# Block 0 of a windowed attention with a gated FFN: scores and PV by 64-key tiles in eight steps

## The chip, the cores and the metric

The kernel runs on one core of a Trainium2 chip. A core has five engines with queues of their own, which meet only through semaphores: TensorE (PE, with its weight loads PEld), VectorE (DVE), ScalarE (ACT), GpSimd (POOL) and SyncE (SP), which here only issues DMAs. TensorE reads SBUF and writes PSUM (eight banks of 128 x 512 float32). The metric is the device time of one execution in microseconds (us), as a median over runs. The trace is one execution taken by the hardware profiler. A line such as L656 is a line of the kernel as it was before the change.

## The reference

The input `x` has 2048 rows of 448 in bfloat16. It is normalized once, and two branches read the result: attention with 16 heads of 28, in which a query sees itself and the 255 keys before it, and a gated FFN of width 1792. Both are added to `x`.

```python
xn = _layernorm(x)
q, k, v = split(xn @ wqkv)                      # 16 heads of 28
scores = einsum("bhqd,bhkd->bhqk", q, k) * 28 ** -0.5
mask = (q_idx - k_idx >= 0) & (q_idx - k_idx < 256)
o = softmax(where(mask, scores, -1e9)) @ v
return x + o.reshape(B, S, D) @ wo + (gelu(xn @ w_gate) * (xn @ w_up)) @ w_down
```

## The kernel before

The rows are worked in four blocks of 512 queries (`qb` 0 to 3). Every queue runs in the order in which the program issues instructions; the order is written out by hand, and nothing is reordered. In each block there are two stages.

*Attention* (`attention`, L617). The heads are worked in four groups `g` of four. A list of steps (`steps_of`, L559) tells which key tiles are scored together. One step scores up to 512 columns for four heads (L684, TensorE, tile `sc`, four PSUM banks of which there is one set), takes the exp of all of it in one ScalarE instruction (L688, tile `p_sb`, five buffers in a ring), and zeroes what lies outside the window. Scores are kept with keys on partitions and queries on columns; the softmax has no maximum, and its denominator comes from a column of ones in `v_sb`. `pv(g)` (L648) multiplies the finished `p_sb` of a group by `v_sb` into PSUM (tile `ov`), and brings it to SBUF as `oc`. `sums` (L625) transposes `oc` on VectorE and takes reciprocals, `inverse` (L633) spreads them, and `scale_o` (L622) multiplies on GpSimd into `oN`.

Blocks 1 to 3 score tiles of 64 keys in two halves of the partitions, in ten steps. Their masks are products with stored 0/1 tiles on VectorE (`apply_masks`, L597, at the start of the step after), and their PV has a bank for each half of the keys: ScalarE copies one to `oc` and VectorE adds the other (`add_halves`, L639). The add of the last group is put off to `flush` (L644).

Block 0 has its own steps: nine, of tiles of 128 keys. Their masks are `affine_select` on GpSimd right after the exp (`masked`, L606), their PV has one bank, copied by VectorE (L666).

Between the steps TensorE is fed other work, from a list `plan` with one entry for each step (L842 for block 0). `(u, 7)` means seven pieces of the generator `u`; a string names one of the functions above. In block 0, `u` is first the projections of groups 1 to 3 (`gen_qk`), then the up projection of five of the seven pairs of FFN columns, in the order p = 1, 2, 3, 0, 4 (`gen_up`, L495: seven pieces a pair; after the seventh, two casts from the tile `ue` to `hT`, both on VectorE, or, for a `p` in `shared`, one on each of VectorE and ScalarE). `w` is the values and projections of block 1 (`gen_pairs`): pairs v0, v2, k0, k1, k2, of seven pieces each. `stat` and `rstd` are the row statistics, `fill_pads` small GpSimd copies into the padding columns of weights. In steps 1 to 3, `ahead`, `ahead2` and `ahead3` normalize rows for the next block on VectorE (L170) and issue DMAs.

PSUM has four spare banks, b0 to b3, in a first-in-first-out list (`take`, `give`, L203): each pair of projections or of FFN columns takes two. A tile on a bank waits until the readers of the tile before it are done.

*FFN* (`gated`, L509). For each `p` a gate projection of 14 matmuls (`gate`, tile `gt`, two sets of two banks, the same PSUM as `sc`), its gelu on ScalarE (L528), and the product with the up projection on VectorE: for `p` in `early` with the stored `hT` (L533), otherwise with PSUM (L536). In block 0 the pairs 0 to 4 are early, so that five gates come one after the other. `gate(0)` also calls `last_v`, which is `rest` (L713): the masks still open, `pv(2)` and `pv(3)`. After each pair, `hook` (L879) issues what belongs to other stages: after pair 0 `sums` of what is open, after pair 1 `inverse`, after pair 4 of block 0 three DMAs of `oN` on the ScalarE queue (`o_collect`, L347, L884). Then ScalarE loads the tables of exp (L899), and the next block's scores take the PSUM of the gates.

Of the kernel before, what the change touches and what calls it, by code (L numbers as in the profile page):

```python
# [27 lines left out]
def kernel(  # L28
# [462 lines left out]
    def both(hT, p):  # L491

        return hT[:, :, :].rearrange("q (h k) n -> q h k n", h=2)[:, :, p, :]
# [15 lines left out]
    def gated(qb, early, last_v, flush, hook):  # L509

        hT = hTs[qb]
        us, ges = {}, {}

        def up(p):
            if p in early:
                return
            us[p] = [take("u") for _ in range(2)]
            for c in range(7):
                chunk(us[p], wu, p, qb, c)

        def gate(p):
            gt = phase[0].pool.tile([P, 2, QB], f32, name="gt", tag="s")
            for c in range(7):
                chunk([gt[:, i, :] for i in range(2)], wg, p, qb, c)
            if not p:
                last_v()
            ges[p] = work.tile([P, 4, QB], bf16, name="p_sb", bufs=5)[:, 0:2, :]
            nc.scalar.activation(out=ges[p][:, :, :], in_=gt[:, :, :], func=ACT.Gelu_apprx_tanh)  # L528

        def end(p):  # L530
            ge = ges.pop(p)
            if p in early:
                nc.vector.tensor_tensor(out=both(hT, p), in0=ge[:, :, :], in1=both(hT, p), op=ALU.mult)  # L533
# [24 lines left out]

    def steps_of(qb):  # L559

        k = 4 * qb
        if not qb:
            def four(g):
                return [(g, None, 3, 384, 128, 0), (g, None, 0, 0, 384, 128)], 512, [(None, (0,), 2 * P, True), (None, (384,), P, False)]

            for g in (0, 2):  # L570
                yield four(g)
                if not g:
                    yield [(0, None, 1, 128, 384, 0), (0, None, 2, 256, 128, 384)], 512, [(None, (0, 384), P, True), (None, (256,), P, False)]
                    yield [(0, None, 2, 384, 128, 0), (1, None, 0, 0, 384, 128)], 512, [(None, (128,), P, True), (None, (384,), P, False)]
                    yield [(1, None, 3, 384, 128, 0), (1, None, 1, 128, 384, 128)], 512, [(None, (0,), 2 * P, True), (None, (384,), P, False)]
                    yield [(1, None, 2, 256, 256, 0), (2, None, 2, 256, 256, 256)], 512, [(None, (0, 256), P, True)]
                else:
                    yield [(2, None, 1, 128, 384, 0), (3, None, 3, 384, 128, 384)], 512, [(None, (0, 384), P, True), (None, (256,), P, False)]
                    yield [(3, None, 0, 0, 384, 0), (3, None, 2, 384, 128, 384)], 512, [(None, (0,), P, True), (None, (256,), P, False)]
                    yield [(3, None, 1, 128, 384, 0), (3, None, 2, 256, 128, 384)], 512, [(None, (0, 384), P, True), (None, (256,), P, False)]  # L580
            return

        def first(g):
            return ([(g, 0, k, 0, 320, 0), (g, 1, k, 64, 320, 0), (g, 0, k - 1, 0, 192, 320), (g, 1, k + 2, 320, 192, 320)], 512, 0)

        def second(g):
            return ([(g, 0, k + 1, 128, 320, 0), (g, 1, k + 1, 192, 320, 0), (g, 0, k + 3, 384, 128, 320), (g, 1, k + 3, 448, 64, 320),
                     (g, 1, k - 2, 0, 128, 384), (g, 0, k - 2, 0, 64, 448)], 512, 1)

        for g in (0, 2):  # L590
            yield first(g)
            yield second(g)
            yield [(g + i, h, k + 2 - 3 * h, 256 - 256 * h, 256, 256 * i) for i in range(2) for h in range(2)], 512, 2
            yield first(g + 1)
            yield second(g + 1)

    def apply_masks(p_sb, i):  # L597

        cols = [c for c, *_ in EDGES[i]]
        for js in ((0,), (1, 2), (3,)):  # L600
            w = 64 * len(js)
            reg = p_sb[:, :, cols[js[0]]:cols[js[0]] + w]
            m = masks[:, i, js[0]:js[-1] + 1, :].rearrange("p a b -> p (a b)").unsqueeze(1).to_broadcast([P, 4, w])
            nc.vector.tensor_tensor(out=reg, in0=reg, in1=m, op=ALU.mult)  # L604

    def masked(p_sb, half, cols, w, diag):  # L606
        r = slice(0, P) if half is None else slice(64 * half, 64 * half + 64)
        for c in cols:
            reg = p_sb[r, :, c:c + w]
            mid = [[0, 4]]  # L610
            if w > P:
                reg = reg.rearrange("p h (b q) -> p h b q", q=P)
                mid.append([0, w // P])
            nc.gpsimd.affine_select(out=reg, in_=reg, pattern=mid + [[1 if diag else -1, min(w, P)]], compare_op=ALU.is_ge, fill=0.0,  # L614
                                    base=0 if diag else -1, channel_multiplier=-1 if diag else 1)

    def attention(qb, plan):  # L617
        oN = blk.tile([P, 4, QB], bf16, name="oN")
# [19 lines left out]

        def add_halves(oc, ov):  # L639
            nc.scalar.copy(out=oc[:, :], in_=ov[0][:, :])  # L640
            nc.vector.tensor_tensor(out=oc[:, :], in0=oc[:, :], in1=ov[1][:, :], op=ALU.add)  # L641
            give(*ov)

        def flush():  # L644
# [2 lines left out]

        def pv(g):  # L648

            ov = [take("ov") for _ in range(2 if qb else 1)]  # L650
            todo = parts.pop(g)
            for n, (half, kt, q0, nq, col, p_sb) in enumerate(todo):
                k0 = 64 * half if half else 0
                r = slice(k0, k0 + (P if half is None else 64))
                for j in range(4):
                    nc.tensor.matmul(ov[half or 0][32 * j:32 * j + 32, q0:q0 + nq], lhsT=v_sb[r, kt, 4 * g + j, :],  # L656
                                     rhs=p_sb[r, j, col:col + nq], start=n == (half or 0), stop=n + len(ov) >= len(todo),
                                     tile_position=(k0, 32 * j), skip_group_check=True)
            oc = work.tile([P, QB], f32, name="oc", tag="wb" if g % 2 else "wa", bufs=1)
            if qb:  # L660
                if g > 2:
                    behind.append((oc, ov))
                else:
# [8 lines left out]
        for i, (scores, ncol, edges) in enumerate(steps):  # L672
# [5 lines left out]
            ss = phase[0].pool.tile([P, 4, QB], f32, name="sc", tag="s")  # L678
            p_sb = work.tile([P, 4, QB], bf16, name="p_sb", bufs=5)
            for g, half, kt, q0, nq, col in scores:  # L680
                k0, nk = (64 * half, 64) if half is not None else (0, P)
                for j in range(4):
                    r = slice(32 * j, 32 * j + Dh)
                    nc.tensor.matmul(ss[k0:k0 + nk, j, col:col + nq], lhsT=kT[r, g, kt * P + k0:kt * P + k0 + nk],  # L684
                                     rhs=qT[r, g, ring(qb).start + q0:ring(qb).start + q0 + nq], start=True, stop=True,
                                     tile_position=(32 * j, k0), skip_group_check=True)
                parts.setdefault(g, []).append((half, kt, q0, nq, col, p_sb))
            nc.scalar.activation(out=p_sb[:, :, 0:ncol], in_=ss[:, :, 0:ncol], func=ACT.Exp, scale=SCALE)  # L688
# [143 lines left out]
    for qb in range(NB):  # L832
# [4 lines left out]
        if qb == 0:  # L837
            new_hT(0)
            early = (0, 1, 2, 3, 4)
            u = chain(gen_qk((1, 2, 3), {1: (3, pvs[3]), 2: (2, pvs[2])}), gen_up(0, (1, 2, 3, 0, 4), (3, 4)))  # L840
            w = gen_pairs(1, (("v", 0), ("v", 2), ("k", 0), ("k", 1), ("k", 2)))
            plan = [[(u, 2), ahead, (u, 1)], [lambda: v_dense(2, pvs[2]), (u, 2), ahead2, (u, 1)],  # L842
                    [lambda: spare.append(spare.pop(1)), (u, 2), ahead3, (u, 4)], [lambda: stat(8), (u, 11)],
                    [lambda: stat(9), (u, 7), lambda: stat(10), (u, 7), lambda: fill_pads(True)], ["sums", (u, 7)],
                    ["inverse", "scale", (w, 11)], [(w, 10)],
                    [lambda: stat(11), (w, 7), lambda: rstd(8, 4), "sums", "inverse", (w, 7)]]
        else:
            d = gen_down(qb - 1)
            if qb < 3:
# [209 lines left out]
```

## Time and profile before

| what | us |
|---|---|
| time, median of 3 runs (212.6 to 213.0) | 212.84 |
| the profiled execution's own time | 212.69 |
| its span, first to last instruction | 210.8 |
| PE busy | 205.1 (97%) |
| DVE busy | 157.8 (75%) |
| ACT busy | 132.0 (63%) |
| POOL busy | 48.4 (23%) |
| the 39 exps (L688), 1878 ns each | 73.2 |
| the 21 selects of block 0 (L614) | 14.2 |

The granted TensorE clock is 1.000 of full speed throughout. Block 0's first scores start at 11.2 us, its last at 33.6; block 1's first start at 51.9.

How to read the rows: in the timeline a row is the start, the length, the engine, the line, the operation, output and input with shapes, and how many instructions were merged. In brackets is the idle time of that engine before it, and what ended it by the profile; where the engine named was done long before, it was something else. "ACTq" and "SPq" are the queues that issue DMAs. Rows of the chain of waits are the start, the length, and what held the end of the kernel in that time. A row of a table of stretches gives the stretch, its length, then for PE, PEld, DVE, ACT and POOL the busy time and the instructions, then the clock, the DMA share and GB/s. Matmuls are pipelined, and two or four of them run in different rows of the array at once, so busy times of one matmul overlap with those of the next.

### The profile page before, as it was taken

The page shows a single profiled execution, that of the slowest core. Times are in us where ns is not written, and L with a number is a line of the kernel's source. Part 1 is how long each engine was busy: PE and PEld are TensorE (multiplying, and loading weights), DVE is VectorE, ACT ScalarE, POOL GpSimd, SP SyncE. Part 2 cuts the span into 40 slices and gives each one's busy share as a digit, 9 for nine tenths or more (in the row PEclk, how much of TensorE's full clock was granted, in tenths as well). Part 3 has the DMA queues.
Part 4 walks back from the last instruction along what each step waited for, and adds up shares of the span by engine and source line. Part 5 has one row for each costly group of instructions (what it writes and reads, how often), then busy time and mean ns, then how long its engine had stood idle before and what let it go on. Part 6 is the DMA issues. An engine that isn't in the chain of part 4 may idle for free.

```text
span 210.8 us, 6335 instructions
## 1 busy us (share of the span) xinstructions
PE 205.1 (97%) x2678; PEld 96.5 (46%) x2682; DVE 157.8 (75%) x356; ACT 132.0 (63%) x124; POOL 48.4 (23%) x83
## 2 busy tenths in 40 slices
PE   7899999999999999999999999999999999999994
PEld 2333444444444445444445444544444454544562
DVE  6899998999788985696438897395385699659722
ACT  4699588566777977413778788523587787757000
POOL 5388658451000220040000112013000022005100
PEclk9999999999999999999999999999999999999999
DMA  6999989959411001003421000100100010100011
GB/s 176 275 223 230 107 215 220 218 175 234 110 48 48 22 5 39 7 3 71 75 75 47 25 0 27 23 0 15 32 3 0 5 47 0 48 3 0 22 59 41
DMA packets 24889, 15.67 MB, mean 74 GB/s; under 512 B 9208, under 2 KB 24728, under 8 KB 24856
## 3 DMA queue, kind: packets, MB, share of 16 engines
q1 hardware_dynamic: 23814, 14.87, 31.7%
q8 instruction: 22, 0.36, 0.7%
q10 hardware_dynamic: 1042, 0.34, 0.6%
q14 instruction: 11, 0.09, 0.1%
HBM read 9.26 MB, written 2.41 MB: 55 GB/s over the span
## 4 chain that ended last, share of the span: by engine, by line
PE 94%; DVE 2%; ACT 1%; DMA 1%; issue 1%; DVEq 0%; ACTq 0%
PE po L394 24%; PE gt L488 20%; PE u L488 12%; PE ue L488 8%; PE sc L684 7%; PE pq L333 7%; PE ov L656 5%; PE pv L319 4%; PE pq L190 2%; PE pl L394 2%; DVE st L155 1%; PE po L403 1%; DMA x_sb<-in_A_x_dram 1%; PE pv L190 1%; ACT p_sb L688 1%; PE s L190 1%
## 5 line engine op out<-in xcount | busy, mean ns | idle before, releaser
L688 ACT ACTIVATE p_sb<-sc 128x2048 bf16<-128x2048 f32 x39 | 73.2, 1878 | 20.0 <-PE sc L684 14.0
L528 ACT ACTIVATE p_sb<-gt 128x1024 bf16<-128x1024 f32 x28 | 28.7, 1025 | 33.6 <-PE gt L488 30.7
L623 POOL TENSOR_TENSOR oN<-oc,l 128x512 bf16<-128x512 f32 x16 | 21.9, 1374 | 117.9 <-DVE l L636 117.9
L488 PE MATMUL gt<-xnT,wg 64*128 64x512 bf16 x224 | 45.6, 376 | 0.0
L394 PE MATMUL po<-wd,hT 128*128 128x448 bf16 x210 | 43.3, 353 | 0.0
L488 PE MATMUL gt<-xsw,wg 64*128 64x512 bf16 x168 | 40.7, 376 | 0.0
L536 DVE TENSOR_TENSOR hT<-p_sb,u 128x512 bf16<-128x512 bf16 x34 | 21.9, 677 | 15.9 <-PE u L488 15.7
L604 DVE TENSOR_TENSOR p_sb<-p_sb,masks 128x256 bf16<-128x256 bf16 (+1 forms) x90 | 27.9, 365 | 7.5 <-ACT p_sb L688 7.5
L394 PEld LDWEIGHTS <-hT 128*128 128x128 bf16 x238 | 21.8, 98 | 19.5 <-issue 2.4
L488 PEld LDWEIGHTS <-wg 64*128 64x128 bf16 x392 | 19.0, 94 | 22.5 <-issue 0.2
L488 PEld LDWEIGHTS <-wu 64*128 64x128 bf16 x392 | 18.7, 94 | 22.5 <-issue 0.8
L488 PE MATMUL u<-xnT,wu 64*128 64x512 bf16 x136 | 28.1, 376 | 0.0
L488 PE MATMUL u<-xsw,wu 64*128 64x512 bf16 x102 | 24.7, 376 | 0.0
L488 PE MATMUL ue<-xnT,wu 64*128 64x512 bf16 x88 | 18.0, 377 | 0.0
L684 PE MATMUL sc<-qT,kT 28*64 28x320 bf16 (+7 forms) x648 | 16.4, 261 | 0.1
L488 PE MATMUL ue<-xsw,wu 64*128 64x512 bf16 x66 | 16.4, 377 | 0.0
L614 POOL TENSOR_SCALAR_AFFINE_SELECT p_sb<-p_sb 128x512 bf16<-128x512 bf16 (+1 forms) x21 | 14.2, 703 | 6.0 <-ACT p_sb L688 5.9
L641 DVE TENSOR_TENSOR oc<-oc,ov 128x512 f32<-128x512 f32 x12 | 8.2, 681 | 9.1 <-ACT oc L640 9.0
L684 PEld LDWEIGHTS <-kT 28*64 28x64 bf16 (+1 forms) x648 | 7.5, 102 | 13.3 <-issue 12.0
L382 DVE TENSOR_TENSOR res<-po,x_sb 128x448 bf16<-128x448 f32 x13 | 7.7, 621 | 7.7 <-PE po L403 4.4
L505 DVE CAST hT<-ue 128x512 bf16<-128x512 f32 x17 | 11.0, 678 | 1.3 <-PE ue L488 1.2
L170 DVE TENSOR_SCALAR xn<-x_sb,mv_all,rstd_all 128x448 bf16<-128x448 bf16 (+1 forms) x28 | 11.0, 434 | 0.3 <-ACT rstd_all L161 0.3
(111 smaller groups left out, 281.2 us busy)
## 6 DMA issues: line engine op xcount, KB each, us to landing
out_dram<-res SPq DMA_DIRECT2D x15, 112.0 KB
wd<-in_B_w_down_dram SPq DMA_DIRECT2D x2, 784.0 KB
x_sb<-in_A_x_dram SPq DMA_DIRECT2D x3, 448.0 KB
xsw<-xnT SPq DMA_DIRECT2D x6, 192.0 KB
wu<-in_B_w_up_dram SPq DMA_DIRECT2D x4, 224.0 KB
wg<-in_B_w_gate_dram SPq DMA_DIRECT2D x2, 448.0 KB
wu<-in_B_w_up_dram SPq DMA_DIRECT2D x2, 336.0 KB
wg<-in_B_w_gate_dram SPq DMA_DIRECT2D x2, 336.0 KB
```

The lines of the kernel that those rows point to most:

```text
L170: nc.vector.tensor_scalar(out=xf[:, lo:lo + n], in0=x_sb[:, t, src:src + n], scalar1=mv_all[:, t, 0:1], scalar2=rstd_all[:, t:t + 1], op0= ...
L333: nc.tensor.matmul(ps, lhsT=w.rearrange("p h d -> p (h d)"), rhs=xchunk(qb, hi, c, qb * QB, QB), start=c == 0, stop=c == 6, tile_position= ...
L394: nc.tensor.matmul(po[:, 0:w], lhsT=x[:, k, tt * P:(tt + 1) * P], rhs=wt[:, k, lo:up], start=start and n == 0, stop=stop and n == len(term ...
L488: nc.tensor.matmul(ps, lhsT=w[64 * hi:64 * hi + 64, c, p * P:(p + 1) * P], rhs=xchunk(qb, hi, c, qb * QB, QB), start=c == 0, stop=c == 6, ...
L505: copy(out=hTs[qb][:, p + 7 * i, :], in_=us[i])
L528: nc.scalar.activation(out=ges[p][:, :, :], in_=gt[:, :, :], func=ACT.Gelu_apprx_tanh)
L536: nc.vector.tensor_tensor(out=hT[:, p + 7 * i, :], in0=ge[:, i, :], in1=u, op=ALU.mult)
L604: nc.vector.tensor_tensor(out=reg, in0=reg, in1=m, op=ALU.mult)
L614: nc.gpsimd.affine_select(out=reg, in_=reg, pattern=mid + [[1 if diag else -1, min(w, P)]], compare_op=ALU.is_ge, fill=0.0, base=0 if diag ...
L623: nc.gpsimd.tensor_tensor(out=oN[:, g, :], in0=oc[:, :], in1=inv, op=ALU.mult)
L684: nc.tensor.matmul(ss[k0:k0 + nk, j, col:col + nq], lhsT=kT[r, g, kt * P + k0:kt * P + k0 + nk], rhs=qT[r, g, ring(qb).start + q0:ring(qb) ...
L688: nc.scalar.activation(out=p_sb[:, :, 0:ncol], in_=ss[:, :, 0:ncol], func=ACT.Exp, scale=SCALE)
```

## The change

Block 0 gets tiles of 64 keys, as the later blocks have them, in two steps for each group, eight in all. In the second step of a group, one more matmul by four heads fills the columns 384 to 512 of the lower half, which hold no score; it is not used in PV.

The masks of steps 1 to 4 stay on GpSimd: now six selects a step, each of 64 partitions by four heads by 64 columns. Those of steps 5 to 8 go to VectorE, with two of the three products that a step of the later blocks has; as there, they are issued at the start of the following step, and those of step 8 in `rest`.

PV of every group has two banks, with a copy on ScalarE and an add on VectorE (448 of the 512 columns, since the upper half of the keys adds nothing to the first 64 queries). The one of group 3 is put off to `flush`, which is now also called after the product of an early pair.

The fills of TensorE are laid out anew over eight steps, with the same pieces in the same order, and of the pair p = 2, which comes second, one cast goes to ScalarE.

```diff
@@ gated / end(p)
             if p in early:
                 nc.vector.tensor_tensor(out=both(hT, p), in0=ge[:, :, :], in1=both(hT, p), op=ALU.mult)
+                flush()
@@ steps_of(0)
-            def four(g):
-                return [(g, None, 3, 384, 128, 0), (g, None, 0, 0, 384, 128)], 512, [(None, (0,), 2 * P, True), (None, (384,), P, False)]
...
-                    yield [(3, None, 1, 128, 384, 0), (3, None, 2, 256, 128, 384)], 512, [(None, (0, 384), P, True), (None, (256,), P, False)]
+            for g in range(4):
+                yield [(g, 0, 0, 0, 320, 0), (g, 1, 0, 64, 320, 0), (g, 0, 2, 256, 192, 320), (g, 1, 2, 320, 192, 320)], 512, 1
+                yield [(g, 0, 1, 128, 320, 0), (g, 1, 1, 192, 320, 0), (g, 0, 3, 384, 128, 320), (g, 1, 3, 448, 64, 320),
+                       (g, 0, 2, 448, 64, 448), (g, None, 3, 384, 128, 384)], 512, 1
@@ apply_masks, masked
-    def apply_masks(p_sb, i):
+    def apply_masks(p_sb, i, n):
-        for js in ((0,), (1, 2), (3,)):
+        for js in ((0,), (1, 2), (3,))[0:n]:
...
+    def masked(p_sb):
+        for hi in range(2):
+            reg = p_sb[64 * hi:64 * hi + 64].rearrange("p h (b q) -> p h b q", q=64)
+            for part, kind in ((reg[:, :, 0], 1), (reg[:, :, 5], 1), (reg[:, :, 4], -1)):
+                nc.gpsimd.affine_select(out=part, in_=part, pattern=[[0, 4], [kind, 64]], compare_op=ALU.is_ge, fill=0.0, base=min(kind, 0),
+                                        channel_multiplier=-kind)
@@ add_halves
-            nc.vector.tensor_tensor(out=oc[:, :], in0=oc[:, :], in1=ov[1][:, :], op=ALU.add)
+            q0 = 0 if qb else 64
+            nc.vector.tensor_tensor(out=oc[:, q0:], in0=oc[:, q0:], in1=ov[1][:, q0:], op=ALU.add)
@@ pv
-            ov = [take("ov") for _ in range(2 if qb else 1)]
+            ov = [take("ov") for _ in range(2)]
...
-            if qb:
-                if g > 2:
-                    behind.append((oc, ov))
-                else:
-                    add_halves(oc, ov)
+            if g > 2:
+                behind.append((oc, ov))
             else:
-                nc.vector.tensor_copy(out=oc[:, :], in_=ov[0][:, :])
-                give(*ov)
+                add_halves(oc, ov)
@@ attention, each step
-            if qb:
-                fresh.append((p_sb, edges))
+            if qb or i > 3:
+                fresh.append((p_sb, edges, 3 if qb else 2))
             else:
-                for m in edges:
-                    masked(p_sb, *m)
+                masked(p_sb)
@@ plan of block 0
-            u = chain(gen_qk((1, 2, 3), {1: (3, pvs[3]), 2: (2, pvs[2])}), gen_up(0, (1, 2, 3, 0, 4), (3, 4)))
+            u = chain(gen_qk((1, 2, 3), {1: (3, pvs[3]), 2: (2, pvs[2])}), gen_up(0, (1, 2, 3, 0, 4), (2, 3, 4)))
...
-                    [lambda: stat(9), (u, 7), lambda: stat(10), (u, 7), lambda: fill_pads(True)], ["sums", (u, 7)],
-                    ["inverse", "scale", (w, 11)], [(w, 10)],
-                    [lambda: stat(11), (w, 7), lambda: rstd(8, 4), "sums", "inverse", (w, 7)]]
+                    [lambda: stat(9), (u, 7), lambda: stat(10), (u, 5), lambda: fill_pads(True)], ["sums", (u, 9)],
+                    ["inverse", "scale", (w, 17)],
+                    [lambda: stat(11), (w, 4), lambda: rstd(8, 4), "sums", "inverse", (w, 14)]]
```

More of the change, by code (lines that the diff above doesn't have):

```diff
@@ L604, in apply_masks @@
             nc.vector.tensor_tensor(out=reg, in0=reg, in1=m, op=ALU.mult)
[L606 to L615, printed above, removed]
+    def masked(p_sb):
[4 more added lines that the diff above has]
+                                        channel_multiplier=-kind)
     def attention(qb, plan):
@@ L648, in pv @@
         def pv(g):
[L650 removed]
+            ov = [take("ov") for _ in range(2)]
             todo = parts.pop(g)
             for n, (half, kt, q0, nq, col, p_sb) in enumerate(todo):
[L653 to L654 removed]
+                k0 = 64 * half
+                r = slice(k0, k0 + 64)
                 for j in range(4):
[L656 to L657 removed]
+                    nc.tensor.matmul(ov[half][32 * j:32 * j + 32, q0:q0 + nq], lhsT=v_sb[r, kt, 4 * g + j, :],
+                                     rhs=p_sb[r, j, col:col + nq], start=n == half, stop=n + 2 >= len(todo),
                                      tile_position=(k0, 32 * j), skip_group_check=True)
             oc = work.tile([P, QB], f32, name="oc", tag="wb" if g % 2 else "wa", bufs=1)
[L660 to L667 removed]
+            if g > 2:
+                behind.append((oc, ov))
+            else:
+                add_halves(oc, ov)
             copied.append((g, oc))
@@ L680, in attention @@
             for g, half, kt, q0, nq, col in scores:
-                k0, nk = (64 * half, 64) if half is not None else (0, P)
+                fills = half is None
+                half = 1 if fills else half
+                k0, nk = 64 * half, 64
                 for j in range(4):
@@ L686, in attention @@
                                      tile_position=(32 * j, k0), skip_group_check=True)
-                parts.setdefault(g, []).append((half, kt, q0, nq, col, p_sb))
+                if not fills:
+                    parts.setdefault(g, []).append((half, kt, q0, nq, col, p_sb))
             nc.scalar.activation(out=p_sb[:, :, 0:ncol], in_=ss[:, :, 0:ncol], func=ACT.Exp, scale=SCALE)
             flush()
-            if qb:
-                fresh.append((p_sb, edges))
-            else:
-                for m in edges:
-                    masked(p_sb, *m)
+            if qb or i > 3:
+                fresh.append((p_sb, edges, 3 if qb else 2))
+            else:
+                masked(p_sb)
             while later:
```

9 lines of the change are left out of this document (removed).

## The prediction

> **What bounds the kernel now.** I read the page first, then the busy time of each engine in stretches of block 0, then the chain that ended last, then each engine's timeline from 9 to 56 us.
>
> ```profile
> PE 205.1 (97%) x2678; PEld 96.5 (46%) x2682; DVE 157.8 (75%) x356; ACT 132.0 (63%) x124; POOL 48.4 (23%) x83
> 26.00:35.00 9.00, 9.00 (x116) 3.75 (x116) 7.58 (x15) 6.95 (x5) 6.52 (x13) 1.00 0.95 214
> 41.00:50.00 9.00, 9.00 (x86) 4.20 (x84) 8.93 (x17) 4.86 (x5) 3.50 (x3) 1.00 0.75 225
> ```
>
> The first row is the page's, the others are stretches (us, then PE, PEld, DVE, ACT, POOL busy). PE is busy 97% of the span and all the time in block 0, so time goes down only with PE's own work, and goes up with any wait put on PE. The second engine to look at is DVE: it has 1.42 us free between 26 and 35, and 0.07 us between 41 and 50. The change adds DVE work in the first of these and a wait in the second, so its place is what matters.
>
> **PE's own work.** From the chain that ended last (start, us, what):
>
> ```profile
> 22.05 0.61 PE ov L656 x20
> 22.65 0.33 PE sc L684 x8
> 22.98 3.13 PE ue L488 x28
> 28.06 0.60 PE ov L656 x16
> 37.15 1.51 PE gt L488 x14
> 38.66 1.10 PE ov L656 x36
> 61.28 1.32 PE pv L319 x14
> 81.60 1.26 PE ov L656 x81
> 155.57 0.34 PE sc L684 x16
> 168.70 0.66 PE ov L656 x40
> 169.36 0.36 PE sc L684 x16
> ```
>
> A step's scores take 0.33 now. The later blocks already use 64-key tiles: 0.34 and 0.36, I take 0.35. Seven pairs take 1.51 (gt), so fourteen take 3.02; the ue stretch has 3.13, so each change over costs 0.11. One step less saves 0.33+0.11 = 0.44, and eight steps at 0.02 more cost 0.16: -0.28 us. PV of a group in block 3 streams 1280 columns in each half in 0.66. The new one streams 1024 and 896 in its halves; 512 columns take 1.51/7 = 0.216, so 256 fewer are 0.11 less: 0.55, against 0.61 and 0.60 for groups 0 and 1 (-0.11). Groups 2 and 3: 1.26-0.22 = 1.04 against 1.10 (-0.06). PE's own work: **-0.45 us**. The fill matmuls of every second step run beside the other half's columns and are in the 0.02. Bounds by the three rows of a step (0.33 to 0.36): -0.61 to -0.37.
>
> **Masks of steps 1 to 4 on POOL.**
>
> ```profile
> 9.41 5.05 POOL L117 TENSOR_SCALAR_AFFINE_SELECT masks<-masks 64x64 bf16<-64x64 bf16 x18
> 14.53 3.47 POOL L614 TENSOR_SCALAR_AFFINE_SELECT p_sb<-p_sb 128x1024 bf16<-128x1024 bf16 x5
> 19.01 1.24 POOL L614 TENSOR_SCALAR_AFFINE_SELECT p_sb<-p_sb 128x512 bf16<-128x512 bf16 x2 [1.00 <-ACT p_sb L688]
> 20.21 0.19 POOL L283 COPY wqp<-wraw 128x16 bf16<-128x16 bf16 x1
> 21.43 0.22 POOL L285 COPY wkp<-wraw 128x48 bf16<-128x48 bf16 x1
> ```
>
> Six selects of 64x256 a step in place of two or three large ones. 64 elements take 5.05/18 = 0.28, 512 take 1.24/2 = 0.62; between them by size, 256 take 0.42 (bounds 0.28 and 0.62), so 2.5 us a step. From 14.53 three steps end at 22.1, the nine fills of wqp and wkp that follow step 3's masks (the first and last row above: 1.4 us) make 23.5, and step 4 ends at 26.0. pv(1) needs that at 28: hidden by 2 us. At 0.62 it would not be (a rival). The same fills are what SP's queue waits for with the weight swap; they end 2 us later than now, ahead of that queue's turn for it, so I cost that at nothing.
>
> **DVE before pv(1).** Timeline rows of DVE; the last two are of block 1 and price a mask:
>
> ```profile
> 20.20 0.61 DVE L155 BATCH_NORM_STATS2 st<-x_sb 128x6 f32<-128x448 bf16 x1
> 20.95 2.45 DVE L505 CAST hT<-ue 128x512 bf16<-128x512 f32 x4
> 26.14 1.29 DVE L505 CAST hT<-ue 128x512 bf16<-128x512 f32 x2
> 27.35 0.70 DVE L629 STREAM_TRANSPOSE l<-oc 128x512 f32<-128x512 f32 x1
> 28.26 0.63 DVE L505 CAST hT<-ue 128x512 bf16<-128x512 f32 x1
> 30.45 1.16 DVE L226 CAST v_sb<-pv 128x448 bf16<-128x448 f32 x2 [0.36 <-PE pv L319]
> 54.73 0.83 DVE L604 TENSOR_TENSOR p_sb<-p_sb,masks 128x256 bf16<-128x256 bf16 x3 [0.63 <-ACT p_sb L688]
> 55.47 0.62 DVE L155 BATCH_NORM_STATS2 st<-x_sb 128x6 f32<-128x448 bf16 x1
> ```
>
> A cast repeats every 0.60, a statistics pair every 0.75, `sums` takes 28.26-27.35 = 0.91. Three masks repeat in 0.74; without one of the two small ones, 0.53 a step. pv now takes two banks, not one, and gives them back only after a ScalarE copy and a DVE add. Followed through the list of spare banks, b0 and b2 go in turn to p=1, pv(0), p=0, pv(1), v2, k1, pv(2), and b1 and b3 to p=2, p=3, p=4, v0, k0, k2, pv(3). So PE waits wherever DVE's reading of the pair before isn't done:
> - pv(0) comes at 22.05 plus four steps' 0.02, 22.13, and needs both casts of p=1 (20.95, 0.60 each, and 0.08 to the end of a cast): 0.1 of wait.
> - pv(1): DVE is free at 26.14 as before (the cast of p=2 that goes to ScalarE pays for the wait on the copy). But then the masks of step 5 (0.53) and `sums` (0.91) stand ahead of p=0's casts, because only five of its seven chunks are issued in step 5; before, its casts came first, at 26.14. They end at 28.27 and 28.87. PE arrives at 28.22 (28.06, +0.08, +0.1, -0.06 for pv(0), two steps' 0.04); the second half waits: 0.65.
> - k0 needs both casts of v0, which stand behind the add of group 1 (to 30.67), the masks of step 6 and the inverse: they end at 32.96, not at 30.45+1.16 = 31.6. PE arrives at 32.37 (pv(1) ends at 29.4, scores 0.35, v0 and v2 1.32 each): 0.63 with the semaphore.
> - k2 needs k0's casts, behind the masks of step 7 and the statistics: 0.1.
>
> Waits: **+1.48** (bounds: nothing, if DVE hands on as it does now, and 2.1, the four pairs of masks added outright). The cover is DVE's 1.42 free; the free time lies at places where DVE has nothing to do, so I take the walk. Gate 0 starts 1.03 later, at 38.2. The last masks end before their PV. ScalarE takes four copies and a cast (0.58 each, row 85.43 below) for one exp (1.88): 1.0 us more in a stretch with 9.00-6.95 = 2.05 free; its exps start up to 0.2 later and still end before PE's next scores, so I cost that at nothing; without that room each 0.2 would count eight times.
>
> **The way out of block 0.**
>
> ```profile
> 41.19 0.70 DVE L629 STREAM_TRANSPOSE l<-oc 128x512 f32<-128x512 f32 x1
> 44.78 2.94 POOL L623 TENSOR_TENSOR oN<-oc,l 128x512 bf16<-128x512 f32 x2 [5.37 <-DVE l L636]
> 41.48 1.02 ACT L528 ACTIVATE p_sb<-gt 128x1024 bf16<-128x1024 f32 x1 [1.46 <-PE gt L488]
> 47.75 1.39 ACTq L350 DMA_DIRECT2D o<-oN  x3
> 49.24 1.02 ACT L528 ACTIVATE p_sb<-gt 128x1024 bf16<-128x1024 f32 x1 [2.21 <-DVE hT L533]
> 50.48 1.02 ACT L528 ACTIVATE p_sb<-gt 128x1024 bf16<-128x1024 f32 x1 [0.22 <-PE gt L488]
> 51.52 1.28 ACT L899 ACT_TABLE_LOAD   x1
> 51.88 0.42 PE L684 MATMUL sc<-qT,kT 28*64 28x320 bf16 x16
> 84.51 1.02 ACT L528 ACTIVATE p_sb<-gt 128x1024 bf16<-128x1024 f32 x1 [0.63 <-PE gt L488]
> 85.43 0.58 ACT L640 COPY oc<-ov 128x512 f32<-128x512 f32 x1
> 86.69 0.68 DVE L641 TENSOR_TENSOR oc<-oc,ov 128x512 f32<-128x512 f32 x1
> ```
>
> Now: `sums` of groups 2 and 3 from 41.19, their inverses, POOL's scaling from 44.78 to 47.72, then ScalarE issues three DMAs of oN (47.75, for 1.39 us), and the gelu of p=5 stands behind them: its wait is named DVE, but its product was done long before; it is the issue. Free time: 0.22 ahead of the last gelu, and 51.88-51.50 = 0.38 before the next block's scores, which take its two banks: 0.60.
> New: group 3's add waits for a ScalarE copy that stands behind the second gelu. Counted from gate 0 (37.15 now): that gelu at 41.48-37.15-0.06 = 4.27, the copy 0.92 later (84.51 to 85.43, the same pair in block 1), 0.58 long, 0.1 to DVE, an add of 448 columns 0.54 (0.68 is for 512 and overlaps the next): `sums` at 6.41 where it was at 4.04. The copy of group 2 also goes ahead of the first gelu, whose bank gate 2 needs at the end of gate 1; that gelu ends some 0.1 us ahead of it, so it costs nothing. Queued behind the add on DVE: `sums`, the next norm and product, the inverses; behind these POOL, the issue, two gelus. 2.37 less 0.60: **+1.75** on the next block's first scores. Bounds: 0 if that queue had another 1.8 us of slack, which no row shows, and 2.37. Afterwards PE is dense and nothing gives the time back.
>
> **Sum.** -0.45+1.48+1.75 = +2.8 us on the profiled execution's 212.69 (span 210.8), which is 0.15 below the median: 212.84+2.8 = **215.6**.
>
> **A port rule weighed.**
>
> ```profile
> 17.50 2.19 DVE L170 TENSOR_SCALAR xn<-x_sb,mv_all,rstd_all 128x448 bf16<-128x448 bf16 x6
> 42.96 0.53 DVE L170 TENSOR_SCALAR xn<-x_sb,mv_all,rstd_all 128x448 bf16<-128x448 bf16 x2
> ```
>
> Three norms take 3x0.53 = 1.6 alone, and 2.19 where POOL's selects run beside some 1.2 us of them (to 18.0, and from 19.0). With POOL selecting without a pause to 26, the same stretch would cost 0.5 more, p=1's casts come 0.5 later, and pv(0) and all behind it with them: 216.1. I leave it out of the sum, since a select half as long may let DVE in sooner. The Trainium skill, "SBUF — State Buffer", section "SBUF: two separate sides", says that VectorE and GpSimd take a shared port pair as an exclusive lock for a whole instruction; the trace agrees in that the norms stretch, and by that rule the sum would be the 216.1.
>
> **Rivals.**
> 1. Only the way out costs, DVE making good its delay in its free time: -0.45+1.75 = +1.3, 214.1. For it: 1.42 us free. Against: the order of the casts. 0.20.
> 2. Only the waits before gate 0 cost: +1.0, 213.9. It needs 1.8 us more slack on ScalarE. 0.07.
> 3. The norms under POOL, above: 216.1. 0.11.
> 4. A select costs 0.62 whatever its size: 3.7 us a step, step 4's masks end at 30.7 and pv(1) starts 1.7 later than forecast, 0.63 of it saved at k0: 216.7. For it: the large selects are all that the trace has on p_sb. Against: 0.28 for 64 elements. 0.05.
> 5. Other side: DVE never holds PE, as its row of 157.8 us against 205.1 would have it, and PE's -0.45 remains: 212.4. It is decided at `sums`: started less than 0.6 us later than now after gate 0, with p=0's casts done by 28.2, the gain stands. Against: 0.07 us of free DVE time from 41 to 50. 0.10.
>
> The forecast has 0.47. The range 213.4 to 216.9 takes in all but 5, with the bounds of the two waits on one side or the other. 0.2% is 0.43 us, about what a measurement of this kernel tells from no change. Rival 5 lies on that edge: 0.06 faster, 0.04 same; the rest, 0.90, slower.
>
> **What would show it.** Scores at 0.35 a step and pv of 36 at 0.55; PE idle before the second PV, waiting for DVE's cast of ue, and before k0; DVE idle 1 us or more after the first hT product, waiting for ScalarE's copy of oc; the three ScalarE issues near 51.2; the scores of block 1 at 54.6. Wrong would be: no idle of PE in block 0, or issues before 48.5.

## The result, and the profile after

The changed kernel takes 215.96 us (median of 4 runs, 215.73 to 216.18), against 212.92 beside it: a ratio of 1.0152 (95% interval 1.0138 to 1.0165), slower by 3.04 us. The prediction was 215.6, slower, in a range from 213.4 to 216.9. The profiled execution's own time is 215.97 (span 214.3), 3.28 us above the 212.69 of the profile before. In what follows the lines of the changed file are: scores L670, exp L675, PV L644, ScalarE's copy of a PV bank L627, VectorE's add L629, masks on VectorE L595, selects L601, `sums` L616 and L617, scaling on GpSimd L610.

The first part of the profile's page and two rows of its groups of instructions (busy time and mean ns; then the idle time just before them and what ended most of it):

```profile
PE 206.6 (96%) x2837; PEld 98.4 (46%) x2842; DVE 158.8 (74%) x363; ACT 132.7 (62%) x128; POOL 43.6 (20%) x86
L670 PE MATMUL sc<-qT,kT 28*64 28x320 bf16 (+4 forms) x736 | 16.2, 259 | 2.0 <-ACT p_sb L528 1.6
L644 PE MATMUL ov<-p_sb,v_sb 64*32 64x320 bf16 (+4 forms) x720 | 11.5, 254 | 0.3 <-DVE hT L505 0.3
```

PE's share fell from 97% to 96%, and the groups name only 1.6 us ahead of scores and 0.3 ahead of PV as idle. So the page of the profile shows 1.9 of the 3 us. The rest lies inside rows that count as busy (PE's busy time grew from 205.1 to 206.6), where a matmul of one half of the array runs alone while the other half waits. It is found by going through PE's timeline of block 0 (start, length, work, idle time before it):

```profile
11.38 0.42 PE L670 MATMUL sc<-qT,kT 28*64 28x320 bf16 x16 [0.17 <-DVE kT L244]
...
22.25 0.88 PE L644 MATMUL ov<-p_sb,v_sb 64*32 64x320 bf16 x36
23.06 0.42 PE L670 MATMUL sc<-qT,kT 28*64 28x320 bf16 x16
23.41 0.39 PE L488 MATMUL ue<-xnT,wu 64*128 64x512 bf16 x1
...
26.11 0.43 PE L670 MATMUL sc<-qT,kT 28*64 28x320 bf16 x24
...
28.61 0.32 PE L644 MATMUL ov<-p_sb,v_sb 64*32 64x320 bf16 x4
29.20 0.56 PE L644 MATMUL ov<-p_sb,v_sb 64*32 64x320 bf16 x32 [0.28 <-DVE hT L505]
29.70 0.42 PE L670 MATMUL sc<-qT,kT 28*64 28x320 bf16 x16
30.05 0.36 PE L319 MATMUL pv<-wv,xnT 64*128 64x448 bf16 x1
...
32.85 0.37 PE L333 MATMUL pq<-xnT,wqp 64*128 64x512 bf16 x1
33.38 0.37 PE L333 MATMUL pk<-xsw,wsq 64*128 64x512 bf16 x1 [0.16 <-DVE v_sb L226]
...
38.37 0.38 PE L488 MATMUL gt<-xnT,wg 64*128 64x512 bf16 x1
...
40.00 1.25 PE L644 MATMUL ov<-p_sb,v_sb 64*32 64x320 bf16 x72
41.18 0.39 PE L488 MATMUL gt<-xnT,wg 64*128 64x512 bf16 x1
...
55.08 0.42 PE L670 MATMUL sc<-qT,kT 28*64 28x320 bf16 x16 [1.64 <-ACT p_sb L528]
```

PV of group 0 takes 23.06-22.25 = 0.81. That of group 1 takes 29.70-28.61 = 1.09: four matmuls of the first half start, and the second half, for which the others wait, gets its bank only at 29.20. The first pair of `k0` starts at 32.85 with one half and at 33.38 with the other. PV of groups 2 and 3 takes 41.18-40.00 = 1.18. Then PE is dense up to block 1's scores, which wait 1.64.

Against the kernel before, whose timeline has block 0's first scores, gate 0 and block 1's first and second scores at these times:

```profile
11.23 0.40 PE L684 MATMUL sc<-qT,kT 28*128 28x128 bf16 x8
...
36.99 0.38 PE L488 MATMUL gt<-xnT,wg 64*128 64x512 bf16 x1
...
51.88 0.42 PE L684 MATMUL sc<-qT,kT 28*64 28x320 bf16 x16
...
54.99 0.43 PE L684 MATMUL sc<-qT,kT 28*64 28x320 bf16 x24
```

| stretch | before | after | more |
|---|---|---|---|
| start of the span to block 0's first scores | 11.23 | 11.38 | 0.15 |
| from there to gate 0 | 25.76 | 26.99 | 1.23 |
| gate 0 to block 1's first scores | 14.89 | 16.71 | 1.82 |
| to block 1's second scores (58.27 after) | 3.11 | 3.19 | 0.08 |

The sum, 3.28, is the whole difference of the two profiled times. From block 1's second scores to the start of the last row of the timeline it is 153.93 before and 154.05 after, in a spread of 153.93 to 154.22 over all profiles of this case. The first row is not the change's: the time of the first scores moved between 11.15 and 11.73 from profile to profile, with edits that lie behind it. So experiments are measured below by one distance, from block 0's first scores to block 1's second ones: 43.76 before and 46.89 after, **3.13 us** apart. This distance has a noise of its own of some 0.2 us: the first PV, 0.81 long here, takes 0.65 to 0.88 in kernels whose edits do not touch it. Where that matters, the part behind gate 0 is given alone: 54.99-36.99 = 18.00 before, 58.27-38.37 = 19.90 after.

What held PE is on VectorE, ScalarE and GpSimd. VectorE's timeline after:

```profile
21.26 1.85 DVE L505 CAST hT<-ue 128x512 bf16<-128x512 f32 x3
...
26.49 0.60 DVE L595 TENSOR_TENSOR p_sb<-p_sb,masks 128x256 bf16<-128x256 bf16 x2
27.02 0.70 DVE L616 STREAM_TRANSPOSE l<-oc 128x512 f32<-128x512 f32 x1
27.76 0.25 DVE L617 RECIPROCAL inv_all<-l 128x16 f32<-128x16 f32 x1
27.93 1.81 DVE L505 CAST hT<-ue 128x512 bf16<-128x512 f32 x3
...
40.19 0.60 DVE L595 TENSOR_TENSOR p_sb<-p_sb,masks 128x256 bf16<-128x256 bf16 x2
...
42.32 0.69 DVE L533 TENSOR_TENSOR hT<-p_sb,hT 128x1024 bf16<-128x1024 bf16 x1 [0.30 <-ACT p_sb L528]
44.44 0.62 DVE L629 TENSOR_TENSOR oc<-oc,ov 128x448 f32<-128x448 f32 x1 [1.43 <-ACT oc L627]
44.98 0.70 DVE L616 STREAM_TRANSPOSE l<-oc 128x512 f32<-128x512 f32 x1
```

The casts of p=0, which free the banks of the second PV, stand at 27.93 behind two masks and `sums`. After the first product VectorE idles 1.43 us until ScalarE has copied group 3's first bank, and only then come `sums`, 44.98-38.37 = 6.61 after gate 0, where they stood 4.20 after it (41.19-36.99). ScalarE's timeline shows where that copy stands, and what the delay becomes:

```profile
42.91 1.02 ACT L528 ACTIVATE p_sb<-gt 128x1024 bf16<-128x1024 f32 x1 [0.62 <-PE gt L488]
43.83 0.58 ACT L627 COPY oc<-ov 128x512 f32<-128x512 f32 x1
...
51.61 1.39 ACTq L350 DMA_DIRECT2D o<-oN  x3
53.09 1.94 ACT L528 ACTIVATE p_sb<-gt 128x1024 bf16<-128x1024 f32 x2 [4.63 <-DMA o<-oN]
55.05 1.28 ACT L885 ACT_TABLE_LOAD   x1
```

The copy follows the second gelu. The three issues of `oN` moved from 47.75 to 51.61, 3.86 later, of which 1.38 is gate 0's own delay. The last two gelus now run without a gap behind the issues, and end at 55.03, when block 1's scores may start.

GpSimd's timeline has the selects:

```profile
14.40 7.38 POOL L601 TENSOR_SCALAR_AFFINE_SELECT p_sb<-p_sb 64x256 bf16<-64x256 bf16 x18
...
23.24 2.37 POOL L601 TENSOR_SCALAR_AFFINE_SELECT p_sb<-p_sb 64x256 bf16<-64x256 bf16 x6
```

That is 7.38/18 = 0.41 each, and step 4's masks end at 25.6, 3 us before the PV that reads them.

### The profile page after: what moved, and what is told of

It reads as the page before. It is cut to its first block, busy times and chain, and to the rows that moved or that the text cites. A ratio compares the mean times of both kernels' runs of the same rounds, so it can differ in the third digit from the quotient of the medians.

```text
span 214.3 us, 6664 instructions
## 1 busy us (share of the span) xinstructions
PE 206.6 (96%) x2837; PEld 98.4 (46%) x2842; DVE 158.8 (74%) x363; ACT 132.7 (62%) x128; POOL 43.6 (20%) x86
## 3 DMA queue, kind: packets, MB, share of 16 engines
HBM read 9.26 MB, written 2.41 MB: 54 GB/s over the span
## 4 chain that ended last, share of the span: by engine, by line
PE 73%; issue 0%; DVE 0%; DVEq 0%
PE po L394 23%; PE gt L488 15%; PE u L488 11%; PE sc L670 5%; PE ue L488 4%; PE pq L333 4%; PE ov L644 4%; PE pv L319 3%; PE pl L394 2%; PE po L403 1%; PE pq L190 1%; PE pq L253 0%; DVE res L382 0%; PE pk L333 0%; PE pl L403 0%
## 5 line engine op out<-in xcount | busy, mean ns | idle before, releaser
L675 ACT ACTIVATE p_sb<-sc 128x2048 bf16<-128x2048 f32 x38 | 71.4, 1878 | 19.1 <-PE sc L670 13.9
L610 POOL TENSOR_TENSOR oN<-oc,l 128x512 bf16<-128x512 f32 x16 | 21.8, 1373 | 132.4 <-DVE l L623 132.4
L595 DVE TENSOR_TENSOR p_sb<-p_sb,masks 128x256 bf16<-128x256 bf16 (+1 forms) x98 | 30.3, 362 | 7.3 <-ACT p_sb L675 7.3
L629 DVE TENSOR_TENSOR oc<-oc,ov 128x512 f32<-128x512 f32 (+1 forms) x16 | 10.6, 666 | 12.7 <-ACT oc L627 12.5
L670 PE MATMUL sc<-qT,kT 28*64 28x320 bf16 (+4 forms) x736 | 16.2, 259 | 2.0 <-ACT p_sb L528 1.6
L670 PEld LDWEIGHTS <-kT 28*64 28x64 bf16 x736 | 8.4, 103 | 14.7 <-issue 12.6
L627 ACT COPY oc<-ov 128x512 f32<-128x512 f32 x16 | 9.4, 584 | 6.0 <-PE ov L644 6.0
L644 PE MATMUL ov<-p_sb,v_sb 64*32 64x320 bf16 (+4 forms) x720 | 11.5, 254 | 0.3 <-DVE hT L505 0.3
L644 PEld LDWEIGHTS <-v_sb 64*32 64x32 bf16 x720 | 8.5, 91 | 6.2 <-issue 4.2
```

Source lines behind the costliest of these rows:

```text
L610: nc.gpsimd.tensor_tensor(out=oN[:, g, :], in0=oc[:, :], in1=inv, op=ALU.mult)
L629: nc.vector.tensor_tensor(out=oc[:, q0:], in0=oc[:, q0:], in1=ov[1][:, q0:], op=ALU.add)
L644: nc.tensor.matmul(ov[half][32 * j:32 * j + 32, q0:q0 + nq], lhsT=v_sb[r, kt, 4 * g + j, :], rhs=p_sb[r, j, col:col + nq], start=n == half ...
```

## The experiments

The theory under test is that of the prediction: PE is held at two separate places, by the order of VectorE's work before gate 0, and by the order of ScalarE's copy and VectorE's add on the way out. Rivals: VectorE simply has too much work (so that less of it would mend both places), or the way out has enough slack for the delay of `sums`, and something else holds block 1's scores.

### Group 3's add at once

```diff
-            if g > 2:
+            if qb and g > 2:
                 behind.append((oc, ov))
```

> Edit: the changed kernel, but in block 0 the halves of group 3 are added right away as for the other groups, not put off behind the second gelu. Theory (the price of the way out is the order: add behind a ScalarE copy behind the second gelu, then sums, inverses, GpSimd's scaling, the three DMA issues on ScalarE, the last two gelus): sums start 1.4 to 1.5 us earlier after gate 0 (43.5 in place of 44.98), the wait of 1.64 us ahead of block 1's first scores falls to about 0.2, gate 2 waits about 0.2 for the first gelu, which now stands behind two copies: 1.3 us faster than the changed kernel, 214.6. Rival (it is VectorE's amount of work that costs, not its order; this edit leaves the amount as it is): 215.9, within 0.3 of the changed kernel.

Measured: 215.24 us (214.95 to 215.67), ratio 1.0128 (1.0111 to 1.0145). Rows of its timelines of VectorE, ScalarE's queue and PE:

```profile
43.77 0.70 DVE L616 STREAM_TRANSPOSE l<-oc 128x512 f32<-128x512 f32 x1
...
50.39 1.39 ACTq L350 DMA_DIRECT2D o<-oN  x3
...
54.18 0.42 PE L670 MATMUL sc<-qT,kT 28*64 28x320 bf16 x16 [0.26 <-ACT p_sb L528]
```

The wait of the scores falls from 1.64 to 0.26, and the distance is 57.37-11.73 = 45.64, 1.25 less than after. Of this, 1.11 lies behind gate 0 (57.37-38.58 = 18.79 against 19.90); the other 0.14 lies ahead of it, where the edit changes nothing. So by the trace the place of ScalarE's copy behind the second gelu carries most of the wait on the way out. By the timed runs the gain is smaller, some 0.5 us by the two ratios, whose intervals just overlap, where 1.3 was expected. The profiled execution, the fastest of the four, is 1.02 faster than the profiled one of the changed kernel; why the other three gain less stays open.

### The three issues of oN on SyncE's queue

```diff
-                o_collect(qb, nc.sync if qb else nc.scalar)
+                o_collect(qb, nc.sync)
```

> Edit: the changed kernel, but block 0's three DMAs of oN are issued by SyncE, not by ScalarE. Theory: the gelu of p=5 no longer stands behind the issues and runs at the end of its gate; the wait of block 1's first scores on the gelus (1.64) goes. VectorE is as late as before, so the products of p=5 and p=6 come to the first output sums of block 1 some 0.6 us late: 1.0 to 1.1 us faster than the changed kernel, 214.9. Rival (VectorE's lateness reaches TensorE through the products anyway, ScalarE's issues are not the door): no gain, 215.9.

Measured: 215.01 us (214.93 to 215.49), ratio 1.0116 (1.0098 to 1.0133). Rows of ScalarE's and PE's timelines of this kernel:

```profile
48.94 1.02 ACT L528 ACTIVATE p_sb<-gt 128x1024 bf16<-128x1024 f32 x1 [0.49 <-PE gt L488]
...
53.36 0.42 PE L670 MATMUL sc<-qT,kT 28*64 28x320 bf16 x16
...
54.58 2.81 PE L394 MATMUL po<-wd,hT 128*128 128x448 bf16 x14 [0.79 <-DVE hT L537]
```

Block 1's scores wait for nothing, and the gelu of p=5 runs at 48.94, right behind its gate's matmuls, where it stood at 53.09. So it was the issues that held the gelus. But the late `sums` still make the last products late, and the first output sum waits 0.79 for one of them: of the 1.64 only 0.78 is gained (57.31-11.20 = 46.11). Behind gate 0 the gain is 0.94 (57.31-38.35 = 18.96 against 19.90), some 0.1 under what was expected, since the wait for the product is 0.79 and not 0.6. The other 0.16 is lost ahead of gate 0, where the edit changes nothing and the first PV took 0.88.

### The casts of p=0 ahead of the sums

```diff
-  ... lambda: fill_pads(True)], ["sums", (u, 9)],
+  ... lambda: fill_pads(True)], [(u, 2), "sums", (u, 7)],
```

> Edit: the changed kernel, with the first sums of block 0 behind the casts of p=0 in VectorE's order (two pieces, sums, seven pieces) and nothing else. Theory: the casts of p=0 end 0.9 us earlier, the second PV of block 0 (28.61 to 29.20) no longer waits: 0.5 us; the later wait ahead of k0 stays, since VectorE's work before v0's casts is the same: 215.45. Rival (the amount of VectorE's work, not its order): 215.9.

Measured: 215.5 us (215.28 to 216.18), ratio 1.0141 (1.0118 to 1.0163). The second PV runs from 28.46 to 29.01 = 0.55, without a wait: the order of casts and `sums` was its cause. But PE's timeline has a new wait right behind it:

```profile
28.46 0.62 PE L644 MATMUL ov<-p_sb,v_sb 64*32 64x320 bf16 x36
...
29.84 0.35 PE L319 MATMUL pv<-wv,xnT 64*128 64x448 bf16 x1 [0.41 <-DMA wsq<-wqp]
```

The name is misleading. What ends there is the cast of p=4 on VectorE (29.16 to 29.79), which now stands behind `sums` in place of p=0's, and whose bank v0 takes; in the last kernel below, the same wait bears VectorE's name. The distance is 57.74-11.22 = 46.52, 0.37 less; the timed runs do not tell this gain from none, as their interval overlaps that of the changed kernel. The wait of block 1's scores is the same 1.64: the two places are independent.

### The masks of steps 5 to 8 on GpSimd

```diff
-            if qb or i > 3:
-                fresh.append((p_sb, edges, 3 if qb else 2))
+            if qb:
+                fresh.append((p_sb, edges, 3))
```

> Edit: the changed kernel, with the masks of steps 5 to 8 on GpSimd too, as those of steps 1 to 4 (six selects a step, some 2.4 us, hidden by some 3 us between steps). VectorE loses four times 0.53 us. Theory: the waits of the second PV (0.55) and of k0 (0.5) go and with them 1.1 us; the way out is as long as it was, since there it is not VectorE's amount that counts: 214.9. Rival (VectorE's amount of work costs everywhere): 2.1 us or more, 213.8 or less. If GpSimd's selects come too late for the third and fourth PV: no gain.

Measured: 214.69 us, ratio 1.0129 (1.0054 to 1.0204); one of its runs lay at 217.44, which makes the interval so wide that the timed runs leave the gain open. It is read from PE's timeline:

```profile
38.98 1.06 PE L644 MATMUL ov<-p_sb,v_sb 64*32 64x320 bf16 x72
...
53.88 0.42 PE L670 MATMUL sc<-qT,kT 28*64 28x320 bf16 x16 [1.64 <-ACT p_sb L528]
```

VectorE has four pairs of masks less. The distance is 57.07-11.44 = 45.63, 1.26 less, of which 1.07 lies ahead of gate 0 (37.36-11.44 = 25.92 against 26.99): the second PV takes 0.63 (28.59 to 29.22), and `k0` hardly waits, while the first PV still takes 0.81. PV of groups 2 and 3 takes 1.00 to the next gate's matmul at 39.98, where it took 1.18: the masks of step 8 (40.19 to 40.79 on VectorE) had held it, which the prediction denied. The wait of the scores is 1.64, to the hundredth what it was. So the rival of too much work falls for the way out: there the order counts, not the amount. Ahead of gate 0 it does not fall: taking work away gave back 1.07 there, and the better order of casts and `sums` 0.54 (37.67-11.22 = 26.45), of which 0.17 was lost again behind gate 0.

### The slack of the way out, measured in the kernel before

One statistics instruction, then four, put ahead of `sums` in the kernel before; what they write is not used.

```diff
+                for _ in range(4 if f == 0 and not qb else 0):      # and range(1 ...
+                    st = work.tile([P, nc.vector.BN_STATS_DIM], f32, name="st")
+                    nc.vector.bn_stats(out=st[:, :], in_=x_sb[:, 0, :])
                 while f == 0 and copied:
```

> Edit: the kernel before the change, with one more batch-statistics instruction on VectorE (0.6 us, its result unused) ahead of the two sums behind gate 0 of block 0. Theory: the sums start 0.6 us later and the way out has 0.60 us of free time (0.22 ahead of the last gelu, 0.38 ahead of the scores): 212.6, no more than 0.1 slower. Rival (no free time: every VectorE delay there reaches the end): 0.6 slower.

> Edit: as the one before, with four of these instructions: the sums start some 2.4 us later, as in the changed kernel, and nothing else of the change is there. Theory: 2.4 less 0.6 = 1.8 us slower than before, 214.4, with the wait of about 1.6 us ahead of block 1's first scores. Rival (the wait is made by something else of the change, the two banks or the copy on ScalarE): within 0.6 us of before.

Measured: with one, 212.79 us, ratio 1.0010 (0.9993 to 1.0028). With four, 214.48 us, ratio 1.0086 (1.0065 to 1.0106). With one, ScalarE's timeline has the issues 0.46 later (0.54 later counted from the first scores, here at 11.15), and no scores wait:

```profile
48.21 1.39 ACTq L350 DMA_DIRECT2D o<-oN  x3
49.70 1.94 ACT L528 ACTIVATE p_sb<-gt 128x1024 bf16<-128x1024 f32 x2 [2.74 <-DVE hT L533]
```

With four, rows of the VectorE and PE timelines:

```profile
41.28 2.20 DVE L730 BATCH_NORM_STATS2 st<-x_sb 128x6 f32<-128x448 bf16 x4
43.39 0.69 DVE L629 STREAM_TRANSPOSE l<-oc 128x512 f32<-128x512 f32 x1
...
53.42 0.42 PE L684 MATMUL sc<-qT,kT 28*64 28x320 bf16 x16 [1.38 <-ACT p_sb L528]
```

Four hold `sums` up by 43.39-41.28 = 2.11. The distance grows by 56.61-11.32-43.76 = 1.53, so 0.58 of the 2.11 is slack, where the prediction had 0.60. A delay of `sums` alone, with nothing else of the change, costs block 1 what lies beyond that slack: this shows the mechanism of the way out by itself. The timed runs give 1.82 for it, 0.3 more than the trace.

### All three together

The first, second and fourth edit at once:

> Edit: the changed kernel with three of its waits taken away: group 3's halves added right away, the masks of steps 5 to 8 on GpSimd, and block 0's three DMAs of oN issued by SyncE. Theory: the waits ahead of the second PV and k0 go (1.1), those of the way out too but for 0.3 at gate 2, which waits for a first gelu behind two copies; TensorE's own 0.45 us remain: 212.6 to 212.9, the same as before within 0.2%. Rival (the 64-key tiles themselves cost, by their number of matmuls): 213.5 or more.

Measured: 213.25 us, ratio 1.0025 (1.0012 to 1.0039), where 212.6 to 212.9 was expected. The distance is 55.45-11.20 = 44.25, 0.49 more than before. Adding group 3 at once puts both copies ahead of the first gelu, and gate 2 waits for that one's banks, as PE's timeline has it:

```profile
41.66 0.37 PE L488 MATMUL gt<-xnT,wg 64*128 64x512 bf16 x1 [0.15 <-ACT p_sb L528]
```

It starts 41.66-39.82 = 1.84 after gate 1, where a gate takes 1.51, so the wait is 0.33, of which the row shows 0.15. The other half of the excess lies ahead of gate 0 (37.21-11.20 = 26.01 against 25.76 before), where the first PV takes 0.82.

The same with that copy on VectorE:

```diff
-        def add_halves(oc, ov):
-            nc.scalar.copy(out=oc[:, :], in_=ov[0][:, :])
+        def add_halves(oc, ov, copy=nc.scalar.copy):
+            copy(out=oc[:, :], in_=ov[0][:, :])
...
-                add_halves(oc, ov)
+                add_halves(oc, ov, nc.vector.tensor_copy if g > 2 and not qb else nc.scalar.copy)
```

> Edit: as the one before, but the first half of group 3 is copied by VectorE, not by ScalarE, so that only one copy stands ahead of the first gelu. Theory: without the 0.3 at gate 2: 212.3 to 212.6, 0.2 to 0.5 faster than before. Rival as above: 213.3 or more.

Measured: 213.12 us, ratio 1.0019 (1.0009 to 1.0029), where 212.3 to 212.6 was expected. The distance is 55.50-11.58 = 43.92, still 0.16 more than before: waits take back what PE's own work gains. The largest is at the first PV, 0.82 long where 0.55 is free of waits:

```profile
22.54 0.89 PE L644 MATMUL ov<-p_sb,v_sb 64*32 64x320 bf16 x36
23.36 0.42 PE L670 MATMUL sc<-qT,kT 28*64 28x320 bf16 x16
```

### The order of VectorE's work, moved further

In the kernel just shown, the statistics of step 4 moved behind the casts of p=1:

```diff
-  [lambda: stat(8), (u, 11)],
+  [(u, 4), lambda: stat(8), (u, 7)],
```

> Edit: as the one with VectorE's copy of group 3, and the statistics of row tile 8 behind the casts of p=1 in VectorE's order instead of ahead of them. Theory: the first PV takes both banks of p=1 and waited some 0.25 us for the second cast (0.82 from its start to the next scores against 0.6); with the casts 0.75 earlier this goes: 0.25 faster than that kernel, 212.9. Rival (what is left over before is TensorE's, by the number of matmuls, not a wait): 213.1.

Measured: 213.17 us, ratio 1.0019 (1.0008 to 1.0029), where 212.9 was expected. The first PV now takes 0.55 (22.18 to 22.73), but PE's timeline has the wait one place on, for the cast of p=2 that the moved statistics hold up:

```profile
23.36 0.37 PE L488 MATMUL ue<-xnT,wu 64*128 64x512 bf16 x1 [0.20 <-DVE hT L505]
```

The distance is 55.12-11.22 = 43.90, no gain. With the first `sums` behind p=0's casts as well, and the inverse behind v0's:

```diff
-  ["sums", (u, 9)], ["inverse", "scale", (w, 17)],
+  [(u, 2), "sums", (u, 7)], [(w, 14), "inverse", "scale", (w, 3)],
```

> Edit: as d_stat, with the first sums behind the casts of p=0, and the first inverse behind the casts of v0. Theory: the rest of the waits ahead of the second PV and k0 (0.2) goes too, TensorE's own 0.42 us show: 212.3 to 212.7, equal to the kernel before or up to 0.4 faster. Rival: 213.1.

Measured: 213.8 us, ratio 1.0042 (1.0028 to 1.0055), where 212.3 to 212.7 was expected. The second PV and k0 wait no more, but PE's timeline shows v0 waiting for p=4's cast, and k2 starts 0.3 later for k0's:

```profile
29.95 0.35 PE L319 MATMUL pv<-wv,xnT 64*128 64x448 bf16 x1 [0.41 <-DVE hT L505]
```

The distance is 55.91-11.32 = 44.59, worse than without these two edits. No version beat the kernel before.

## Why the prediction was right, and where its terms were off

**PE's own work, predicted -0.45.** A step's scores take 23.41-23.06 = 0.35 and 0.36 (26.11 to the next matmul at 26.47), 0.02 to 0.03 more than before; with one step less (0.44) that is some -0.20 where -0.28 was predicted. PV where nothing holds it takes 0.55 as predicted, and groups 2 and 3 take 0.99 to 1.00 in the kernels without step 8's masks on VectorE (predicted 1.04). Together -0.20-0.11-0.11 = -0.42. Right.

**Waits before gate 0, predicted +1.48.** By the same durations of a matmul as in the prediction:

| wait | predicted | measured | from |
|---|---|---|---|
| pv(0) | 0.1 | 0.26 | 0.81-0.55 |
| pv(1) | 0.65 | 0.63 | 1.09-0.55, and 0.09 before its start: 28.61-26.11 = 2.50, of which scores 0.36, nine pieces 1.94 and a change over 0.11 are 2.41 |
| k0 | 0.63 | 0.64 | three pieces and a change over are 0.76, the stretch from 32.85 to the scores at 34.11 is 1.26, so 0.50 (a piece is 0.216); and 0.14 before 32.85: fourteen pieces of 0.19 from 30.05 |
| k2 | 0.1 | 0 | its halves start at 36.86 and 36.90 |

The sum is 1.53. The walk through the list of banks gave the two large waits within 0.02 us. The first was mis-sized: p=1's casts start at 21.26, 0.16 later than before on the same base (20.95+0.15), and the prediction had left them at the old time. Of the 0.16, some 0.13 arises at the statistics ahead of them, which start 0.73 after the cast before (19.77 to 20.50), and 0.60 after it in the kernel before (19.60 to 20.20); what holds them is not shown. With PE's own -0.31 of that stretch these make 1.22 of the 1.23 measured. The forecast for it was 1.48-0.45 = +1.03, which counted in the 0.06 of groups 2 and 3 that lies behind gate 0; the other 0.14 of the difference are pv(0)'s 0.16 and 0.08 of PE's steps, less k2's 0.1.

**"The last masks end before their PV"** was wrong. PV of groups 2 and 3 takes 1.18, not 1.04, and 0.99 once these masks are off VectorE: about 0.2 us, for which the sum had nothing.

**The way out, predicted +1.75.** The copy behind the second gelu, `sums` 2.41 later relative to gate 0 (predicted 2.37), the issues at 51.61 (51.2, with a gate 0 that came 0.2 earlier), the slack of 0.58 (0.60): each step is in the trace, and taking away either the order of the copy or the place of the issues took all or most of the wait of block 1's scores off. That `sums` came out within 0.04 is in part luck: the second gelu came 4.54 after gate 0 (42.91-38.37), 0.11 later than forecast on the same base (4.27+0.16), because of the longer PV, and the way from the copy to the add took 0.61 (43.83 to 44.44) where 0.68 had been counted. Measured: gate 0 to block 1's scores +1.82, in which the 0.08 of the PV above lies.

**Sum.** Predicted +2.8; measured 1.23+1.82+0.08 = 3.13 between the profiles without the head, 3.04 by the timed runs. The forecast was right in sign, place and mechanism. The rest, 0.3, is pv(0) (0.16), the masks of step 8, and the own work of a step (0.08), less k2; 0.08 between block 1's first and second scores stay open.

**The rivals.** Only the way out, or only the waits before gate 0: fell, both are there, and each goes without the other. The norms slowed under GpSimd's selects: fell. VectorE's timeline of the changed kernel has

```profile
17.72 2.14 DVE L170 TENSOR_SCALAR xn<-x_sb,mv_all,rstd_all 128x448 bf16<-128x448 bf16 x6
```

so the norms take 2.14 with GpSimd selecting the whole time, as against 2.19 with selects beside part of them, and 1.6 alone: they are slowed, but no more than before. Of that rival's 0.5 us, p=1's casts show the 0.16 named above at most, whatever held them. By the Trainium skill, "SBUF — State Buffer", section "SBUF: two separate sides", whichever of VectorE and GpSimd starts first has the shared port pair for its whole instruction. The extra 0.5 us that the prediction worked out by that rule did not appear in the norms here. A select of 0.62 whatever its size: fell, 0.41. That VectorE never holds PE: fell, since `sums` started 2.41 later after gate 0, where it allowed 0.6.

## What to carry to other kernels

When a dense engine hands PSUM banks round, follow the banks and not the busy shares: VectorE did 1.0 us more in all (158.8 against 157.8), and PE waited 1.5 us before gate 0 for casts that stood behind masks and `sums`. Moving casts ahead gave back 0.37 in all, taking the masks off VectorE 1.26: with as little VectorE time free as here, order alone moved waits more than it removed them. A delay on a second engine costs what goes beyond the slack of the whole chain behind it, and that slack can be measured by putting idle work into the old kernel, as with the four statistics. An instruction that waits in an in-order queue, as the DMA issue on ScalarE did here until 51.61, holds everything behind it (two gelus), so ask first what stands behind it.

## What was not expected of the hardware

GpSimd selecting without a pause from 14.40 to 21.78 slowed VectorE's norms beside it no more than selects beside part of them had (2.14 against 2.19). The profile books only part of a wait when the matmul of one half of the array is already running: of 0.63 before and in the second PV it shows 0.28 as idle, and of 0.64 at k0 it shows 0.16. Where instructions of VectorE were only moved, a wait taken off at one pair of banks came back at the next, in part or whole, three times out of three: 0.54 at the second PV came back as 0.41 at v0, 0.27 at the first PV as 0.20 at the next up projection, and k0's as 0.3 at k2.
